# When the gate and up weights of the next feed-forward tiles are asked for

## The chip, the cores and the metric

The kernel runs on one core of a Trainium2 chip. A core has a matmul engine (PE, with its weight loads shown apart as PEld), a vector engine (DVE), a scalar engine (ACT), a general-purpose engine (POOL), and a queue processor (SP) that here only issues DMAs. The metric is device time in microseconds (us), the median of several runs. All arithmetic is on 4-byte floats; large matmuls are done in three parts (high by high, high by low, low by high) of operands that were split into a high and a low part.

## The reference

One transformer block over 2048 rows of 512 features, with modulation vectors made from a condition `c`:

```
mod = silu(c) @ w_mod                      # six vectors of 512: sa, ca, ga, sb, cb, gb
h = layernorm(x) * (1 + ca) + sa
x = x + ga * (softmax(q k^T / 4) v) @ wo   # 32 heads of 16 features, q, k, v = h @ wqkv
h = layernorm(x) * (1 + cb) + sb
x = x + gb * (silu(h @ w_gate) * (h @ w_up)) @ w_down    # 512 -> 1792 -> 512
```

## The kernel before, in words

The 2048 rows are cut into four chunks of 512. First q, k and v are projected. Then attention runs over 32 units: a unit is one chunk of query rows (4) by one group of four heads (8), in 16 steps of 128 keys. For each step PE computes four score blocks (L573), ACT takes their exponentials (L575), and PE multiplies them with v (L588, "pv"). Beside that, 21 steps ahead, PE computes the scores once more in another orientation (L524) and DVE takes their row maxima (L526); one score block and one maximum block form a "pair" in `pair_of`. The finished maxima of a unit go into two rows of its query operand `qop` by eight small DMAs (L563, `qop<-turned`) or two (L542, `qop<-mr`), and the unit's first score needs them.

When a unit ends, `close_unit` sends off its sum row (L599, `dn<-o`), and asks for the keys and queries of the unit three further on (L448, `kop<-kd` and `qop<-qd`, one half from SP's queue and one from POOL's). Some steps later the reciprocal goes out (L604, `d_dr<-dn`), comes back spread over partitions (L609, `rb<-d_dr`), and POOL multiplies it in (L614).

When all eight units of a chunk are done, the chunk's output projection, second layer norm and feed-forward follow, mixed into the attention of the next chunk. For chunks 0 to 2 this is done by `filled_tile` and `filled`: they issue 16 (or 8) pairs and between them, by a table of places, the matmuls of one feed-forward tile; behind the pairs stands a block of pv matmuls. The feed-forward has 14 gate-and-up tiles of 128 features (`gate_up`, 0 to 13) and 7 pairs of down tiles (`down`). The order of the jobs is gate_up 0, 1, 2, two downs, gate_up 3, 4, two downs, 5, 6, and so on to 13. A gate-and-up tile is 48 matmuls in row halves (L790 in `accumulate`). Its weights, high and low parts together, are 1 MB, and were written to DRAM in that form earlier.

The tile `wgu` that holds these weights has two buffers in turn (`tile_gu`, `bufs=2`); the two tiles of output-projection weights (`load_wo`) use the same two. `load_gu(f)` takes the next buffer and issues the DMA `wgu<-gu_dr` from SP's queue (L718); it does nothing where tile f was already asked for:

```
def load_gu(self, f):
    if f < NF and f not in self.loaded:
        self.loaded.add(f)
        self.w[f] = self.places[f % len(self.places)] if self.places else tile_gu()
        nc.sync.dma_start(self.w[f].bitcast(F32), gu_dr[f])
```

The DMA waits, on SP, until the last matmul that read the buffer's earlier contents has ended; whatever SP has behind it in program order waits too. Each engine runs its instructions in the order in which this program writes them. `gate_up(ch, f, ...)` begins with `ch.load_gu(f + ch.ahead)`, and `ahead` is 1 for chunks 0 to 2; `scaled`, which starts the second layer norm, loads tile 0. The last chunk runs alone at the end, with `ahead` 4 and more buffers, and with whole rows instead of halves. The down weights (`load_wd`, L723, 1 MB) have one buffer and are asked for at the end of the second down of the pair before.

Of the kernel before, what the change touches and what calls it, by code (L numbers as in the profile page):

```python
# [104 lines left out]
def block_kernel(ctx, tc, x, wqkv, wo, w_gate, w_up, w_down, c, w_mod, out):  # L105
# [526 lines left out]
    def tile_mid():  # L632
        return pf.tile([P, 2, CW], F32R, name="mid", tag="mid", bufs=3)

    def tmp(name):
        return pf.tile([P, CW], F32, name=name, tag="tmp", bufs=4)
# [142 lines left out]
    def accumulate(outs, lhs, rhs, nk, after, halves, by_k=False, trade=False):  # L779
        ends = []  # L780


        terms = [(k, a, b) for k in range(nk) for a, b in ((0, 0), (0, 1), (1, 0))]
        z = len(terms) - 1
        if halves:
            for ph in range(2):
                for j, (k, a, b) in enumerate(terms):
                    for e in (ph, 1 - ph):
                        rows = slice(64 * (ph ^ e), 64 * (ph ^ e) + 64)
                        mm = nc.tensor.matmul(outs[e], lhs(e, a, k)[rows], rhs(b, k)[rows],  # L790
                                              start=(ph == 0 and j == 0), stop=(j == z and (ph == 1 or trade)),
                                              skip_group_check=(ph == 1 and trade))
                        if trade and j == z * (1 - ph):
                            if ph == 0:
                                ends.append(mm.ins.name)
                            else:
                                tc.add_manual_dep(mm.ins, seen.ins.name, SYNC, reason="row halves trade banks")
                    if trade and j == z and ph == 0:
                        seen = nc.scalar.nop()
                        for name in ends:  # L800
                            tc.add_manual_dep(seen.ins, name, SYNC, reason="row halves trade banks")
                    if j == z and ph:
                        after()
                    yield
        else:
            order = [(e, j) for e in range(2) for j in range(z + 1)]
            for e, j in sorted(order, key=lambda o: o[1] // 3) if by_k else order:
                k, a, b = terms[j]
                nc.tensor.matmul(outs[e], lhs(e, a, k), rhs(b, k), start=(j == 0), stop=(j == z))  # L809
                if e == 1 and j == z:  # L810
                    after()
                yield
# [42 lines left out]
    def gate_up(ch, f, outs, halves, trade=False):  # L855
        ch.load_gu(f + ch.ahead)
        if f == 0:
            ch.load_wd(0)
        ch.mid[f] = mid = tile_mid()

        def after():
            th = tmp("th")
            nc.scalar.activation(th, outs[0], AF.Tanh, scale=0.5)  # L863

            def later():
                q = tmp("q")
                nc.vector.scalar_tensor_tensor(q, th, 1.0, outs[0], op0=ALU.add, op1=ALU.mult)  # L867
                m32 = tmp("m32")
                nc.vector.tensor_mul(m32, outs[1], q)  # L869
                slow = halves or (ch.ci, f) == (last - 1, NF - 2)  # L870
                (nc.gpsimd.tensor_copy if slow else nc.scalar.copy)(mid[:, 0, :], m32)  # L871
                (nc.gpsimd if slow else nc.vector).tensor_sub(mid[:, 1, :], m32, mid[:, 0, :].bitcast(F32))  # L872
            posts.append(later)

        w = ch.w.pop(f)
        return accumulate(outs, lambda e, a, k: w[:, 2 * e + a, k, :], lambda b, k: ch.hT[b][:, k, :], NK, after,
                          halves, trade=trade)
# [29 lines left out]

    def scaled(ch):
        ch.load_gu(0)
        ch.norm_scale(nc.gpsimd)  # L910
        ch.nt = [tile_mid().bitcast(F32) for _ in range(2)]
        for t in range(4):
            ch.normalize(t)
# [65 lines left out]
    halves = [(i, half) for i in range(n) for half in range(2)]  # L979
# [118 lines left out]
    for ci in range(last):  # L1098
        plain(STARTS[ci] - done // 4)
        ch = chunks[ci]  # L1100
        for t0 in (0, 2):
            filled_tile(out_pair, ch, t0)
        behind.append([6, lambda: scaled(ch)])
        tails = [None] * 10
        for k in range(NK):
            tails += [lambda tp, k=k: ch.turned(tp, k), None, None]
        plain(NORM, tails)
        if ci == last - 1:
            plain(REST)
        for _ in range(len(ch.jobs) - (KEEP if ci == last - 1 else 0)):  # L1110
            job, args = ch.jobs.pop(0)
            if ci == last - 1 and args == (7,):
                plain(18 - REST)
            if job is gate_up:
                filled_tile(job, ch, *args)
            else:
                filled(DOWN, job(ch, *args, outs, True))
# [25 lines left out]
    ch, chp = chunks[last], chunks[last - 1]  # L1143
# [54 lines left out]
```

## Time and profile before

| | us |
|---|---|
| median of 3 runs | 1848.37 (1847.08 to 1849.05) |
| the profiled execution, its own time | 1851.1 |
| span of its trace, first to last instruction | 1849.3 |
| PE busy | 1815.8 (98% of the span) |
| DVE busy | 1508.7 (82%) |
| ACT busy | 1234.1 (67%) |
| POOL busy | 459.3 (25%) |
| mean granted clock of PE | 0.991 |

Times in the trace count from the span's start. The chain of waits follows the work that ended last backwards; its shares say which engine or DMA held the end at each moment. In the tables of stretches each row is one stretch of time: its length, the busy time of each engine with the number of its instructions in brackets, the clock granted to PE (1.00 is full), the share of the 16 DMA engines in use, and GB/s. Matmuls on the two row halves run side by side, so PE starts more of them than their single durations would allow. In this profile the landings of DMAs issued by SP are not listed; when a load has landed is seen from the instruction that waited for it, or from the DMA share.

### The profile page before, as it was taken

The page shows a single profiled execution, that of the slowest core. Times are in us where ns is not written, and L with a number is a line of the kernel's source. Part 1 is how long each engine was busy: PE and PEld are TensorE (multiplying, and loading weights), DVE is VectorE, ACT ScalarE, POOL GpSimd, SP SyncE. Part 2 cuts the span into 40 slices and gives each one's busy share as a digit, 9 for nine tenths or more (in the row PEclk, how much of TensorE's full clock was granted, in tenths as well). Part 3 has the DMA queues.
Part 4 walks back from the last instruction along what each step waited for, and adds up shares of the span by engine and source line. Part 5 has one row for each costly group of instructions (what it writes and reads, how often), then busy time and mean ns, then how long its engine had stood idle before and what let it go on. Part 6 is the DMA issues. An engine that isn't in the chain of part 4 may idle for free.

```text
span 1849.3 us, 41033 instructions
## 1 busy us (share of the span) xinstructions
PE 1815.8 (98%) x16892; PEld 1180.7 (64%) x16892; DVE 1508.7 (82%) x2558; ACT 1234.1 (67%) x2356; POOL 459.3 (25%) x538
## 2 busy tenths in 40 slices
PE   9999999999999899989999899989999999999999
PEld 7876444444464677767564677767564577677887
DVE  6478999999999788878999788878999988932543
ACT  4223888888888666656788666656788876774211
POOL 3622544655223111111133111111123111130200
PEclk9999999999999999989999999999999999999999
DMA  9784866677645444445445444445443555233642
GB/s 310 277 236 139 215 182 164 175 183 197 190 77 121 99 122 109 113 111 139 107 121 120 99 107 122 115 110 141 105 121 79 130 118 137 109 121 121 267 171 109
DMA packets 80704, 267.63 MB, mean 145 GB/s; under 512 B 19884, under 2 KB 24428, under 8 KB 59836
## 3 DMA queue, kind: packets, MB, share of 16 engines
q1 hardware_dynamic: 61540, 179.71, 33.4%
q0 software_dynamic: 18288, 84.49, 19.0%
q8 instruction: 133, 2.18, 0.5%
q10 hardware_dynamic: 688, 0.80, 0.1%
q14 instruction: 55, 0.45, 0.1%
HBM read 201.85 MB, written 62.13 MB: 143 GB/s over the span
## 4 chain that ended last, share of the span: by engine, by line
PE 79%; DVE 14%; DMA 5%; ACT 1%; issue 0%; SPq 0%; DVEq 0%; ACTq 0%
PE bank L588 20%; PE bank L790 19%; DVE mx L526 14%; PE bank L573 13%; PE bank L524 11%; PE bank L809 8%; PE bank L214 7%; DMA wgu<-gu_dr 4%; PE bank L852 1%; DMA dn<-o 1%; DMA wm_ab<-in_w_mod 1%; PE bank L773 0%; PE bank L166 0%; DVE v_flat L883 0%; ACT o L592 0%
## 5 line engine op out<-in xcount | busy, mean ns | idle before, releaser
L526 DVE TENSOR_REDUCE mx<-bank 128x1 f32<-128x512 f32 x2048 | 1261.1, 681 | 146.8 <-PE bank L524 81.5
L573 PE MATMUL bank<-qop,kop 50*128 50x512 f32 x2048 | 735.5, 429 | 2.2 <-ACT pu__13024 L575 0.5
L524 PE MATMUL bank<-kop,qop 48*128 48x512 f32 x2048 | 728.5, 427 | 1.0 <-DVE mx L526 0.5
L573 PEld LDWEIGHTS bank<-qop,kop 50*128 50x128 f32 x2048 | 348.3, 185 | 195.8 <-issue 35.3
L524 PEld LDWEIGHTS bank<-kop,qop 48*128 48x128 f32 x2048 | 348.8, 186 | 111.1 <-DVE mx L526 67.6
L790 PE MATMUL bank<-act,wgu 64*128 64x512 f32 x1872 | 314.7, 402 | 21.5 <-DMA wgu<-gu_dr 21.5
L790 PEld LDWEIGHTS bank<-act,wgu 64*128 64x128 f32 x1872 | 195.9, 192 | 42.4 <-issue 23.1
L614 POOL TENSOR_TENSOR rb<-o,rb 128x512 f32<-128x512 f32 x31 | 39.8, 1285 | 430.1 <-DMA rb<-d_dr 378.9
L871 POOL CAST mid<-m 128x512 fp32r<-128x512 f32 x40 | 24.2, 606 | 475.1 <-DVE m L869 475.1
L790 PE MATMUL bank<-wd,mid 64*128 64x512 f32 x912 | 131.1, 391 | 0.0
L790 PEld LDWEIGHTS bank<-wd,mid 64*128 64x128 f32 x912 | 91.0, 186 | 12.1
L214 PE MATMUL bank<-hT,wqs 128*128 128x512 f32 x384 | 94.3, 397 | 0.4 <-DVE wqs L354 0.4
L214 PEld LDWEIGHTS bank<-hT,wqs 128*128 128x128 f32 x384 | 70.6, 188 | 18.9 <-issue 3.0
L867 DVE SCALAR_TENSOR_TENSOR q<-th,bank 128x512 f32<-128x512 f32 x56 | 37.8, 676 | 54.5 <-ACT th L863 54.5
L863 ACT ACTIVATE th<-bank 128x512 f32<-128x512 f32 x56 | 33.5, 598 | 58.7 <-PE bank L809 58.5
L883 DVE TENSOR_TENSOR x<-bank,x 128x512 f32<-128x512 f32 x84 | 53.9, 685 | 16.1 <-PE bank L790 16.1
L869 DVE TENSOR_TENSOR m<-bank,q 128x512 f32<-128x512 f32 x56 | 38.7, 692 | 21.4 <-PE bank L809 19.4
L872 POOL TENSOR_TENSOR mid<-m,mid 128x512 fp32r<-128x512 f32 x40 | 51.3, 1282 | 3.4
L809 PE MATMUL bank<-wd,mid 128*128 128x512 f32 x216 | 51.3, 393 | 0.0
L214 PE MATMUL bank<-wqs,hT 128*128 128x512 f32 x192 | 48.0, 398 | 0.0
L790 PE MATMUL bank<-wgu,act 64*128 64x512 f32 x288 | 47.8, 392 | 0.0
L809 PEld LDWEIGHTS bank<-wd,mid 128*128 128x128 f32 x216 | 40.4, 188 | 8.9
(6300 smaller groups left out, 5140.9 us busy)
## 6 DMA issues: line engine op xcount, KB each, us to landing
wgu<-gu_dr SPq DMA_DIRECT2D x48, 1024.0 KB
wd<-wd_dr SPq DMA_DIRECT2D x28, 1024.0 KB
kop<-kd SPq DMA_DIRECT2D x33, 768.0 KB
kop<-kd POOLq DMA_DIRECT2D x29, 768.0 KB, 8.6
gu_dr<-wgu POOLq DMA_DIRECT2D x14, 1024.0 KB, 13.5
kd<-prt SPq DMA_DIRECT2D x16, 512.0 KB
qd<-prt SPq DMA_DIRECT2D x16, 512.0 KB
kop<-gu_dr SPq DMA_DIRECT2D x8, 1024.0 KB
```

The source lines that it names most:

```text
L214: nc.tensor.matmul(pt, lhs(a, k), rhs(b, k), start=(n == 0), stop=(n == 3 * nk - 1))
L524: nc.tensor.matmul(pm, qop[u][rows, s, qt * P:(qt + 1) * P], kop[u % 3][rows, s, kc * CW:(kc + 1) * CW], start=True, stop=True)
L526: nc.vector.tensor_reduce(mx[u][:, b, s, qt, kc:kc + 1], pm, op=ALU.max, axis=AX.X)
L573: nc.tensor.matmul(sp, kop[u % 3][rows, h // 2, kt * P:(kt + 1) * P], qop[u][rows, h // 2, :], start=True, stop=True)
L588: nc.tensor.matmul(pv[u][32 * h:32 * h + 32, cols], v_flat[:, e0:e0 + 32], p_[h][:, cols], start=(kt == 0 and half == 0), stop=(kt == 15), ...
L614: mul.tensor_mul(rb, o, rb)
L790: mm = nc.tensor.matmul(outs[e], lhs(e, a, k)[rows], rhs(b, k)[rows], start=(ph == 0 and j == 0), stop=(j == z and (ph == 1 or trade)), sk ...
L809: nc.tensor.matmul(outs[e], lhs(e, a, k), rhs(b, k), start=(j == 0), stop=(j == z))
L867: nc.vector.scalar_tensor_tensor(q, th, 1.0, outs[0], op0=ALU.add, op1=ALU.mult)
L869: nc.vector.tensor_mul(m32, outs[1], q)
L872: (nc.gpsimd if slow else nc.vector).tensor_sub(mid[:, 1, :], m32, mid[:, 0, :].bitcast(F32))
L883: nc.vector.tensor_add(ch.x2[:, t, :], outs[e], ch.x2[:, t, :])
```

## The change

In the tiles that are done in row halves (chunks 0 to 2), `after`, which is called when the last matmul of tile f has been issued, first asks for tile f + 2. That load takes the buffer that tile f has just read. `scaled` asks for tile 1 right behind tile 0. The call at the head of `gate_up` stays; in these chunks it finds its tile already asked for. The number of loads and of all other instructions stays the same.

```
--- before
+++ after
@@ gate_up
         ch.mid[f] = mid = tile_mid()
 
         def after():
+            if halves:
+                ch.load_gu(f + 2)
             th = tmp("th")
             nc.scalar.activation(th, outs[0], AF.Tanh, scale=0.5)
...
@@ scaled
     def scaled(ch):
         ch.load_gu(0)
+        ch.load_gu(1)
         ch.norm_scale(nc.gpsimd)
```

The first place that the prediction speaks of is the start of chunk 0's feed-forward in SP's queue. The weight loads are `wgu<-gu_dr`, the down weights `wd<-wd_dr`, and `kop`/`qop` the keys and queries of a later unit. Before (tile 0's load is the row ahead of these):

```order
L599 DMA dn<-o 128x1x16
L448 DMA kop_88<-kd 48x2x2048
L448 DMA qop<-qd 48x2x512
L604 DMA d_dr<-dn 128x16
L609 DMA rb<-d_dr 128x1x512
L718 DMA wgu<-gu_dr 128x2048
L723 DMA wd<-wd_dr 128x2048
L563 DMA qop<-turned 2x8x32 x8
L599 DMA dn<-o 128x1x16
L448 DMA kop_971<-kd 48x2x2048
L448 DMA qop<-qd 48x2x512
L718 DMA wgu<-gu_dr 128x2048 x2
```

And now:

```order
L718 DMA wgu<-gu_dr 128x2048 x2
L599 DMA dn<-o 128x1x16
L448 DMA kop_88<-kd 48x2x2048
L448 DMA qop<-qd 48x2x512
L604 DMA d_dr<-dn 128x16
L609 DMA rb<-d_dr 128x1x512
L723 DMA wd<-wd_dr 128x2048
L563 DMA qop<-turned 2x8x32 x8
L718 DMA wgu<-gu_dr 128x2048
L599 DMA dn<-o 128x1x16
L448 DMA kop_971<-kd 48x2x2048
L448 DMA qop<-qd 48x2x512
```

Tile 1's load has moved up to tile 0's, away from the place ahead of `wd`. Tile 2's load has moved from behind `dn<-o`, `kop_971<-kd` and `qop<-qd` (where it stood with tile 3's) to ahead of them, right behind the eight small writes.

The second place is the middle of chunk 0's feed-forward in the same queue, between the loads of tiles 6 and 10. Before:

```order
L718 DMA wgu<-gu_dr 128x2048 x2
L563 DMA qop<-turned 2x8x32 x8
L599 DMA dn<-o 128x1x16
L448 DMA kop_88<-kd 48x2x2048
L448 DMA qop<-qd 48x2x512
L723 DMA wd<-wd_dr 128x2048
L718 DMA wgu<-gu_dr 128x2048
L604 DMA d_dr<-dn 128x16
L609 DMA rb<-d_dr 128x1x512
L718 DMA wgu<-gu_dr 128x2048
L563 DMA qop<-turned 2x8x32 x8
```

And now:

```order
L718 DMA wgu<-gu_dr 128x2048
L563 DMA qop<-turned 2x8x32 x8
L718 DMA wgu<-gu_dr 128x2048
L599 DMA dn<-o 128x1x16
L448 DMA kop_88<-kd 48x2x2048
L448 DMA qop<-qd 48x2x512
L723 DMA wd<-wd_dr 128x2048
L604 DMA d_dr<-dn 128x16
L718 DMA wgu<-gu_dr 128x2048
L609 DMA rb<-d_dr 128x1x512
L718 DMA wgu<-gu_dr 128x2048
L563 DMA qop<-turned 2x8x32 x8
```

In the first of these two pieces the loads are those of tiles 6 and 7 together, then 8, then 9; in the second they are those of tiles 7, 8, 9 and 10. Tile 10's load, which before came only after the next `kop<-kd`, is now ahead of the second block of eight small writes.

More of the change, by code (lines that the diff above doesn't have):

```diff
@@ L861, in after @@
         def after():
+            if halves:
+                ch.load_gu(f + 2)
             th = tmp("th")
@@ L909, in scaled @@
         ch.load_gu(0)
+        ch.load_gu(1)
         ch.norm_scale(nc.gpsimd)
```

## The prediction

> **What bounds the kernel now.** I read the page first, then the waits, then the chain of waits, then tables of stretches around what they point at.
>
> ```profile
> span 1849.3 us, 41033 instructions
> ...
> PE 1815.8 (98%) x16892; PEld 1180.7 (64%) x16892; DVE 1508.7 (82%) x2558; ACT 1234.1 (67%) x2356; POOL 459.3 (25%) x538
> ...
> PE 79%; DVE 14%; DMA 5%; ACT 1%; issue 0%; SPq 0%; DVEq 0%; ACTq 0%
> PE bank L588 20%; PE bank L790 19%; DVE mx L526 14%; PE bank L573 13%; PE bank L524 11%; PE bank L809 8%; PE bank L214 7%; DMA wgu<-gu_dr 4%; PE bank L852 1%; DMA dn<-o 1%; DMA wm_ab<-in_w_mod 1%; PE bank L773 0%; PE bank L166 0%; DVE v_flat L883 0%; ACT o L592 0%
> ```
>
> PE is busy for all but 33.5 us of the span, and 79% of the chain is PE's own work. The one DMA with a share to speak of is the load of gate and up weights, 4%. The waits say what PE loses to it:
>
> ```profile
> PE bank L790 <- DMA wgu<-gu_dr: 21.5, 4, 5.7
> ```
>
> Four waits, 21.5 us together, the longest 5.7: nearly two thirds of all of PE's idle time. The other loads of this kind cost PE nothing. The first of the four, in SP's timeline and (the last two rows) in the chain:
>
> ```profile
> 615.95 0.60 SPq L599 DMA_DIRECT2D dn<-o  x1
> 616.66 0.42 SPq L448 DMA_DIRECT2D kop<-kd  x1
> 617.16 0.38 SPq L448 DMA_DIRECT2D qop<-qd  x1
> 617.64 7.58 SPq L718 DMA_DIRECT2D wgu<-gu_dr  x2
> ...
> 617.64 16.82 DMA wgu<-gu_dr
> ...
> 634.60 1.65 PE bank L790 x6
> ```
>
> Tile 2's weights are asked for at 617.64, behind a unit's keys and queries, and take 16.82 us to land. PE starts the tile at 634.60. The other three waits are tile 10 of chunk 0 and tiles 2 and 10 of chunk 1, the places where a unit closes just before the load is issued. In chunk 2 the units close at other points.
>
> The wait is not all that is lost. This table of 2 us stretches has PE's granted clock in the third column from the right:
>
> ```profile
> 630.00:632.00 2.00, 0.00 (x0) 0.00 (x0) 0.47 (x1) 0.23 (x1) 0.00 (x0) 1.00 0.96 358
> 632.00:634.00 2.00, 0.00 (x0) 0.00 (x0) 0.00 (x0) 0.00 (x0) 0.00 (x0) 0.67 0.99 414
> 634.00:636.00 2.00, 1.40 (x6) 1.24 (x8) 0.00 (x0) 0.00 (x0) 0.00 (x0) 0.50 0.52 217
> 636.00:638.00 2.00, 2.00 (x12) 1.69 (x10) 0.73 (x2) 0.60 (x2) 0.00 (x0) 0.50 0.01 4
> 638.00:640.00 2.00, 2.00 (x14) 1.64 (x14) 1.41 (x3) 1.28 (x3) 0.00 (x0) 0.62 0.00 0
> 640.00:642.00 2.00, 2.00 (x20) 1.40 (x18) 1.92 (x4) 1.67 (x4) 0.00 (x0) 1.00 0.00 0
> ```
>
> While PE waits, its clock falls to half, and it comes back only some 5 us after PE has resumed: 12 matmuls start in 2 us where 20 do at the full clock.
>
> **The change part by part.** What a stall costs in all is read from equal pieces of work: from the start of the tile ahead of the stall to the start of the first down behind the stalled tile, that is two gate-and-up tiles with their pairs and pv blocks. The four stalled pieces and two clean ones (the second and third row):
>
> ```profile
> 615.78:650.18 34.40, 29.15 (x292) 21.08 (x289) 22.95 (x38) 18.77 (x36) 4.85 (x7) 0.90 0.55 127
> 663.79:690.50 26.71, 26.71 (x291) 19.24 (x288) 22.47 (x37) 18.97 (x36) 4.82 (x6) 1.00 0.62 135
> 744.44:771.06 26.62, 26.62 (x290) 19.46 (x288) 22.97 (x41) 18.53 (x36) 5.02 (x6) 1.00 0.44 143
> 784.67:820.11 35.44, 29.76 (x290) 21.60 (x288) 22.94 (x38) 18.78 (x36) 3.58 (x4) 0.86 0.56 138
> 1031.62:1066.27 34.65, 29.41 (x291) 21.43 (x288) 22.85 (x37) 18.77 (x36) 4.85 (x7) 0.90 0.56 126
> 1201.61:1236.59 34.98, 29.67 (x290) 21.57 (x288) 22.94 (x37) 18.77 (x36) 3.57 (x4) 0.90 0.56 138
> ```
>
> All hold 290 to 292 matmuls. A clean piece takes 26.7 us with PE busy throughout; the stalled ones take 7.7, 8.7, 7.9 and 8.3 us more, **32.6 us** together: 21.5 of waiting and 11.1 of half clock. In a clean piece DVE is busy for 22.9 of 26.7 us and ACT for 19.0, so PE stays the bound when the stall is gone, and DVE has 3.8 us to spare.
>
> The Trainium skill (TensorE: Matmul & The Clock Gate, Part 1) says that after an idle window of about 3.4 us PE runs at half clock, and prices this as the throttled time times one half. The mean clocks 0.90, 0.86, 0.90 and 0.90 above make 30.7 us of throttled time, so by that rule 15.4 us on top of the 21.5, or 36.9, and the median would become 1811.5. The trace agrees on the half clock; it gives 11.1 because part of each slow stretch lies inside the wait, where nothing is slowed.
>
> *Tile 2's load*, now asked for at the end of tile 0. When that is, and when tile 8 of chunk 0 ends, which now releases tile 10's load, is in the rows of L790 for these two tiles (first and last start):
>
> ```profile
> L790 PE MATMUL bank<-act,wgu x48: 384/392/399, 602.3 to 611.1; 64*128 64x512 f32 x48
> ...
> L790 PE MATMUL bank<-act,wgu x48: 385/392/400, 757.7 to 766.4; 64*128 64x512 f32 x48
> ```
>
> Tile 0 has ended by 611.5, so the load is issued then instead of at 617.64, and goes ahead of the keys. It is needed when tile 1 has run its course, half a clean piece after 615.8, at 615.8 + 13.3 = 629.1. Its length has two bounds. Alone, a load moves like tile 0's, issued at 564.51:
>
> ```profile
> 564.00:566.00 2.00, 2.00 (x26) 0.93 (x26) 2.00 (x5) 1.87 (x5) 0.00 (x0) 1.00 0.37 61
> 566.00:568.00 2.00, 2.00 (x31) 0.90 (x22) 1.93 (x6) 1.65 (x5) 0.25 (x2) 1.00 0.88 344
> 568.00:570.00 2.00, 2.00 (x24) 0.90 (x18) 2.00 (x5) 1.71 (x5) 1.41 (x8) 1.00 0.31 131
> ...
> 610.00:612.00 2.00, 2.00 (x24) 1.57 (x24) 2.00 (x5) 1.90 (x4) 0.00 (x0) 1.00 0.00 0
> 614.00:616.00 2.00, 2.00 (x30) 1.20 (x24) 0.23 (x1) 0.66 (x2) 1.91 (x3) 1.00 0.00 0
> ```
>
> 2 us times (61 + 344 + 131) GB/s is the 1 MB: it is over by 570, about 5 us. Behind a unit's keys it took 16.82. So it lands between 616.5 and 628.3; even the late end is 0.8 us ahead of the need. I take 5 to 6 us, since the last two rows show the DMA engines empty where it now goes. *Tile 10's load* is released at 766.4 + 0.4 and needed, one clean tile behind 784.67, at 798: with 16.8 us it would still be 14 us early. Chunk 1 has the same order. So all four waits go, and with them the half clock: -32.6, with an end of -21.5 if the slow clock had another cause.
>
> *Tile 1's load* moves beside tile 0's at a chunk's start. It adds 5 us of DMA ahead of `dn<-o`, `kop` and `qop`, and takes 5 us away ahead of `wd`. Nothing waits on the first three there, and the rows above show the engines drained by 570; cost 0, and at most the same 5 us, three times, if a keys' load were just in time, which no wait on `kop` or `qop` by PE shows.
>
> *The other loads* of tiles 3, 7, 9 and 11 are issued where they were, those of 4, 5, 6, 8, 12 and 13 earlier, ahead of keys, `rb` or `wd`. PE waited for none of them; what they are put ahead of can come at most one load, 5 us, later. Keys have time (no wait of PE on them), `wd` is asked for two gate-and-up tiles, 26.7 us, before its down: 0.
>
> *What SP now holds up.* A load that waits for its tile's last matmul holds whatever is behind it. Behind tile 4's and tile 12's loads stands `rb<-d_dr`, which then lands some 5 us later. POOL waits for it; its next work:
>
> ```profile
> 651.06 1.30 POOL L614 TENSOR_TENSOR rb<-o,rb 128x512 f32<-128x512 f32 x1 [0.75 <-DMA rb<-d_dr]
> ...
> 675.26 0.60 POOL L871 CAST mid<-m 128x512 fp32r<-128x512 f32 x1 [22.01 <-DVE m L869]
> ```
>
> 22 us of idle POOL cover that; 0. Without that cover 5 us would fall on `mid` and the downs. The eight writes L563 are tighter, since a unit's first score needs them:
>
> ```profile
> SPq L563 <- DMA wgu<-gu_dr: 3.7, 6, 1.8
> ...
> 1079.99 6.10 SPq L563 DMA_DIRECT2D qop<-turned  x8
> ...
> 1087.47 0.47 PE L573 MATMUL bank<-qop,kop 50*128 50x512 f32 x1 [0.52 <-ACT pu__13024 L575]
> ```
>
> Here the writes waited 1.8 us for tile 4's load just ahead, ended at 1086.1, and the score behind them came 0.5 us late. In the change that load is asked for a tile earlier and only `wd` stands ahead of the writes: 0.5 won back. Two places a chunk (tiles 7 and 10, in chunk 2 four) keep a load just ahead of the writes, as before the change; with 5 us a load they are where they were, 0.
>
> **Sum**: 32.6 + 0.5 = 33.1. The profiled execution took 1851.1 for a span of 1849.3, so its successor should take 1818.0. The median is 2.7 below that execution: 1848.4 - 33.1 = **1815.3 us**, 1.8% faster.
>
> **The rivals.**
>
> *The slow clock stays (0.04).* Then only the waits go: 1848.4 - 21.5 - 0.5 = 1826.4. For it: no row names the cause of the half clock. Against it is the mean over the whole span:
>
> ```profile
> core 0: 1849.3 us, clock 0.991
> ```
>
> The four pieces lack 0.10 x 34.40 + 0.14 x 35.44 + 0.10 x 34.65 + 0.10 x 34.98 = 15.4 us of clock, 0.008 of the span. That leaves 0.001 for all the rest, so the slow clock comes with the stalls only.
>
> *Only tile 10's waits go (0.04).* Tile 2's load has only tile 1's time to land, and the 0.8 us at the late end is thin. If keys delay it all the same, 7.7 + 7.9 stay: 1815.3 + 15.6 = 1830.9. Against it: it is now ahead of the keys.
>
> *The gain is given back (0.02).* A later stage with DVE as its bound could absorb time: the chain has 14% on L526. Then the time is near 1848. Against: DVE works on what PE has written, so its work moves forward with PE's.
>
> *Slower (0.03).* SP's queue becomes the bound through the eight writes. Eight times in the three chunks they stand right behind a load, and SP already waits in such loads:
>
> ```profile
> SPq L718 <- PE bank L573: 78.2, 10, 11.0
> ```
>
> If those loads took 16.8 instead of 5 us, each unit's first score would come 16.8 - 5 - 1.4 (1086.1 to 1087.47) = 10.4 us late: 83 us in all. It decides from 33.1 / 8 = 4.1 us a place; at half the places the time is 1815.3 + 42 = 1857. Against: at the same places a load stands ahead of the writes already, and the six waits there come to 3.7 us. The Trainium skill (DMA: Bandwidth & Descriptors, Anatomy of one DMA) speaks for this rival: DMA engines do not wait on semaphores, the issuing sequencer does, before dispatch. The 78.2 us agree.
>
> **How the numbers follow.** The forecast holds 0.87. With the rivals, faster by over 0.2% (about what a measurement of this kernel tells from no change) is 0.95, within it 0.02, slower 0.03. The forecast's own range is 1811.5 to 1819, by the half clock's price and the run's spread; the first rival widens it to 1828. The second and the rest, 0.09, stay out.
>
> **What would show it.** Right: no wait of L790 on `wgu<-gu_dr`, a mean clock of 0.99 to 1.00 with no stretch at half inside the feed-forwards, the tile pairs at 26.7 us, tile 2's load issued within 1 us of tile 0's end. Wrong: waits of L573 behind L563, L871 late behind L614, or a clock that still falls to half.

## The result, and the profile after

| | median, us | from to, runs |
|---|---|---|
| before | 1848.26 | 1847.08 to 1849.05, 6 |
| after | 1818.11 | 1816.22 to 1820.13, 6 |

The ratio is 0.9838, with a 95% interval of 0.9825 to 0.9851: 30.2 us less. The forecast was 1815.3, with a range of 1811.5 to 1828. The profiled execution of the changed kernel took 1817.3, where the forecast for it was 1818.0.

The page of the changed kernel, the lines that answer to those of before:

```profile
span 1815.5 us, 41028 instructions
...
PE 1804.4 (99%) x16892; PEld 1171.6 (65%) x16892; DVE 1508.9 (83%) x2558; ACT 1233.2 (68%) x2356; POOL 458.9 (25%) x538
...
PE 86%; DVE 12%; DMA 1%; ACT 1%; issue 0%; SPq 0%; DVEq 0%
...
L790 PE MATMUL bank<-act,wgu 64*128 64x512 f32 x1872 | 305.7, 392 | 0.0
```

PE's idle time fell from 33.5 to 11.1 us, and DMA from 5% of the chain to 1%. The last line, of the costliest groups, is the one to look at (busy time, mean duration in ns, idle time of PE ahead of it). The same line of the page of before:

```profile
L790 PE MATMUL bank<-act,wgu 64*128 64x512 f32 x1872 | 314.7, 402 | 21.5 <-DMA wgu<-gu_dr 21.5
```

The idle time of PE ahead of gate-and-up matmuls, 21.5 us before, is 0.0. The same 1872 matmuls also take 392 ns in the mean instead of 402: that is the half clock that is gone. Over all its work PE is busy for 11.4 us less (1815.8 to 1804.4), close to the 11.1 us of half clock in the prediction's sum.

SP's timeline of the changed kernel at the first of the four places, and (last row) the mean granted clock of the whole span:

```profile
610.70 0.33 SPq L718 DMA_DIRECT2D wgu<-gu_dr  x1
615.18 0.61 SPq L599 DMA_DIRECT2D dn<-o  x1
615.84 0.46 SPq L448 DMA_DIRECT2D kop<-kd  x1
616.35 0.42 SPq L448 DMA_DIRECT2D qop<-qd  x1
624.08 0.34 SPq L718 DMA_DIRECT2D wgu<-gu_dr  x1
...
core 0: 1815.5 us, clock 1.000
```

Tile 2's load now leaves at 610.70, as tile 0's last matmul ends, 4.5 us ahead of SP's next DMA. How long it takes is seen from the DMA engines (the last two columns, share in use and GB/s), which were empty until then:

```profile
608.00:610.00 2.00, 2.00 (x20) 1.56 (x18) 2.00 (x5) 1.80 (x4) 0.00 (x0) 1.00 0.00 0
610.00:612.00 2.00, 2.00 (x32) 1.28 (x32) 2.00 (x4) 1.85 (x4) 0.00 (x0) 1.00 0.36 61
612.00:614.00 2.00, 2.00 (x44) 1.23 (x40) 0.96 (x2) 0.00 (x0) 0.78 (x2) 1.00 0.77 295
614.00:616.00 2.00, 2.00 (x25) 1.36 (x17) 1.01 (x2) 1.44 (x3) 2.00 (x3) 1.00 0.42 176
```

2 us times (61 + 295 + 176) GB/s is about its 1 MB, so it is over by about 616. The four pieces of work that were stalled before, each again from the start of the tile ahead to the start of the down behind:

```profile
615.00:641.68 26.68, 26.68 (x292) 19.31 (x288) 22.68 (x38) 18.63 (x36) 4.82 (x7) 1.00 0.71 156
776.18:802.86 26.68, 26.68 (x290) 19.34 (x288) 22.57 (x37) 18.56 (x36) 3.55 (x4) 1.00 0.73 173
1014.32:1041.01 26.69, 26.69 (x290) 19.24 (x288) 22.55 (x38) 18.56 (x36) 4.81 (x7) 1.00 0.72 155
1175.62:1202.34 26.72, 26.72 (x291) 19.27 (x289) 22.57 (x38) 18.62 (x36) 3.57 (x4) 1.00 0.74 173
```

All four take the 26.7 us of a clean piece, at full clock.

### The profile page after: what moved, and what is told of

Read it like the earlier page. It is cut to its first block, busy times and chain, and to the rows that moved or that the text cites. A ratio compares the mean times of both kernels' runs of the same rounds, so it can differ in the third digit from the quotient of the medians.

```text
span 1815.5 us, 41028 instructions
## 1 busy us (share of the span) xinstructions
PE 1804.4 (99%) x16892; PEld 1171.6 (65%) x16892; DVE 1508.9 (83%) x2558; ACT 1233.2 (68%) x2356; POOL 458.9 (25%) x538
## 4 chain that ended last, share of the span: by engine, by line
PE 86%; DVE 12%; DMA 1%; ACT 1%; issue 0%; SPq 0%; DVEq 0%
PE bank L588 22%; PE bank L790 20%; PE bank L573 15%; PE bank L524 12%; DVE mx L526 12%; PE bank L809 8%; PE bank L214 7%; PE bank L852 1%; DMA wm_ab<-in_w_mod 1%; PE bank L773 1%; PE bank L166 0%; DMA qop<-mr 0%; DVE v_flat L885 0%; PE bank L538 0%; SPq L255 0%
## 5 line engine op out<-in xcount | busy, mean ns | idle before, releaser
L524 PEld LDWEIGHTS bank<-kop,qop 48*128 48x128 f32 x2048 | 346.1, 184 | 109.0 <-DVE mx L526 66.4
L790 PE MATMUL bank<-act,wgu 64*128 64x512 f32 x1872 | 305.7, 392 | 0.0
L790 PEld LDWEIGHTS bank<-act,wgu 64*128 64x128 f32 x1872 | 190.3, 186 | 17.9
L790 PE MATMUL bank<-wd,mid 64*128 64x512 f32 x912 | 131.3, 391 | 0.0
L790 PEld LDWEIGHTS bank<-wd,mid 64*128 64x128 f32 x912 | 91.3, 186 | 11.8
L865 ACT ACTIVATE th<-bank 128x512 f32<-128x512 f32 x56 | 33.5, 598 | 58.4 <-PE bank L809 58.2
L885 DVE TENSOR_TENSOR x<-bank,x 128x512 f32<-128x512 f32 x84 | 53.9, 685 | 16.1 <-PE bank L790 16.1
L790 PE MATMUL bank<-wgu,act 64*128 64x512 f32 x288 | 47.7, 392 | 0.0
```

What stands on the lines that cost most here:

```text
L524: nc.tensor.matmul(pm, qop[u][rows, s, qt * P:(qt + 1) * P], kop[u % 3][rows, s, kc * CW:(kc + 1) * CW], start=True, stop=True)
L885: nc.vector.tensor_add(ch.x2[:, t, :], outs[e], ch.x2[:, t, :])
```

## The experiments

Times are compared with the kernel before on the same chip: 1848.9 for the first four, 1847.3 for the next four, 1848.1 for the last three.

**The parts of the change.** Each one alone:

```
last_slot_only:  the change without    +  ch.load_gu(1)   in scaled
tile1_only:      of the change only    +  ch.load_gu(1)   in scaled
tile2_only:      of the change only    +  if halves and f == 0:  ch.load_gu(f + 2)
tile10_only:     of the change only    +  if halves and f == 8:  ch.load_gu(f + 2)
```

> Only the load at the last slot of each tile, without asking for tile 1 beside tile 0. My theory (the gain is the four waits for tiles 2 and 10 and the half clock behind them): all of the gain, 32 to 33 us, some 1816 to 1818, no wait of L790 on wgu. The rival that asking for tile 1 early matters: less gain by 5 us or more, with a wait left at tile 1 or 2.

> Only tile 1 beside tile 0 at a chunk's start, the rest as before. My theory: no gain, 1848 within 1 us, the four waits stay as they are (5.2 to 5.7 us each). Rival: tile 2's waits get shorter because tile 1's load is out of the way, 1848 less up to 15 us.

> The load at the last slot for tile 0 alone, so only tile 2 is asked for early. My theory: the two waits of tile 2 go with their half clock, 7.7 + 7.9 = 15.6 us, some 1832.7; tile 10's two waits stay. If stalls only moved on to the next place: 1848.

> The load at the last slot for tile 8 alone, so only tile 10 is asked for early. My theory: the two waits of tile 10 go, 8.7 + 8.3 = 17.0 us, some 1831.3, and this gain and that of tile 2 alone add up to that of the whole change within 1.5 us. If they hide each other: a sum well off 32.6.

| | median, us | ratio to before, 95% interval |
|---|---|---|
| last slot only | 1817.8 | 0.983 (0.9816 to 0.9845) |
| tile 1 only | 1849.4 | 1.000 (0.999 to 1.001) |
| tile 2 only | 1832.8 | 0.9913 (0.9898 to 0.9927) |
| tile 10 only | 1831.7 | 0.9908 (0.9893 to 0.9923) |

The load at the last slot is the whole gain; asking for tile 1 beside tile 0 is worth nothing, as expected. The early loads of tile 2 and of tile 10 bring 16.1 and 17.2 us, 33.3 together against 31.1 for all tiles on the same chip. The sum is 2.2 us off, more than the 1.5 that I had allowed, but the 95% interval of each of these gains reaches some 2.7 us either way. Within that the gains add, and no other load is seen to matter. The stalls that were left in the two partial kernels (two pieces of tile 2 only, then two of tile 10 only) show something else:

```profile
776.10:808.86 32.76, 28.35 (x291) 20.46 (x289) 22.70 (x37) 18.57 (x36) 3.58 (x4) 0.95 0.59 148
1182.35:1217.06 34.71, 29.37 (x291) 21.38 (x288) 22.82 (x38) 18.75 (x36) 3.56 (x4) 0.90 0.58 141
```
```profile
614.14:648.25 34.11, 28.96 (x292) 21.03 (x289) 22.92 (x38) 18.77 (x36) 4.82 (x7) 0.90 0.56 128
1020.95:1054.77 33.82, 28.67 (x291) 20.83 (x288) 22.82 (x38) 18.67 (x36) 4.83 (x7) 0.90 0.57 130
```

They cost 6.1, 8.0, 7.4 and 7.1 us over a clean piece: 28.6 together, where the same four cost 32.6 in the trace of before. The waits differ little (PE waited 9.7 and 10.3 us in these two traces, 20.0 together, against 21.5); the stretch of half clock varies more. At the first of them the mean clock was 0.95, at the same place before 0.86.

**Was the load asked for too late, or only behind the wrong thing?** In this kernel the weights are asked for as before, but the keys go behind them at the four unit ends.

```
 in close_unit, for u in (10, 13, 18, 21):
-    load_k(u + 3); load_q(u + 3)
+    at(i + 3, lambda: (load_k(u + 3), load_q(u + 3)))
```

> The kernel before, with weights asked for when they were, but at the four unit ends ahead of the stalls the next keys and queries (L448) are asked for three steps later, behind the weight load. If the load was late because the keys stood ahead of it: the load lands about 5 us after its issue at 616 to 617, the four waits go, 1815 to 1818. If one tile of lead is too short by itself: the waits stay, 1848.

Measured: 1820.4, ratio 0.9856 (0.9842 to 0.9871). In SP's timeline of this kernel, and its waits (last row):

```profile
615.34 0.42 SPq L718 DMA_DIRECT2D wgu<-gu_dr  x1
615.81 0.42 SPq L448 DMA_DIRECT2D kop<-kd  x1
616.28 0.58 SPq L448 DMA_DIRECT2D qop<-qd  x1
...
PE bank L790 <- DMA wgu<-gu_dr: 1.3, 3, 0.8
```

One exchange of rows in a queue takes 27 us off, although the load leaves hardly earlier than before (0.7 us behind `dn<-o`, where it was 1.7). But my reason was only half right. I expected it to land in 5 us; PE still waited for such loads three times, 1.3 us in all, and at the first of them the tile began at 628.21, 12.9 us after the issue, where it took 16.8 before. The keys' other half goes through POOL's queue at the same moment (it left at 614.51), and SP ran on and issued its own half at once, since nothing made it wait three steps. So the load shared the DMA engines from its first moment, where the change has them to itself for over 4 us (POOL's half leaves there at 615.05).

**Is the half clock a price of PE standing idle?** Here the kernel before gets extra matmuls ahead of the four stalled tiles, whose results the tile overwrites.

```
 in gate_up:
+    if halves and ch.ci < 2 and f in (2, 10):
+        for _ in range(24):        # 12 in the second kernel
+            nc.tensor.matmul(outs[0], ch.hT[0][:, 0, 0:P], ch.hT[0][:, 0, :], start=True, stop=True)
```

> The kernel before, with 24 extra matmuls of 128x512 (about 5.2 us at full clock) ahead of tiles 2 and 10 of chunks 0 and 1, into a bank that the tile then starts anew. They fill PE's wait for the weights. If the half clock comes from PE standing idle: clock 1.00 throughout, each stalled piece 5.3 to 6 us longer than a clean one instead of 7.7 to 8.7, some 1837 to 1839. If it comes from something else (the DMA load, say): the half clock stays and the time is 1848 or above.

> As with 24, but 12 extra matmuls (2.6 us), so that PE still waits about 2.8 us at each of the four places. If only a wait longer than about 3 us costs the clock: as with 24, 1837 to 1839. If any wait of some us does: the half clock stays, some 1847 to 1849.

| | median, us | ratio to before, 95% interval |
|---|---|---|
| 24 extra matmuls | 1841.8 | 0.9967 (0.9955 to 0.9979) |
| 12 extra matmuls | 1841.4 | 0.9971 (0.9958 to 0.9983) |

Work that nobody needs made the kernel faster. The first stalled piece with 24 of them:

```profile
615.67:648.24 32.57, 32.57 (x314) 23.46 (x312) 22.80 (x38) 18.64 (x36) 4.80 (x7) 1.00 0.60 135
```

PE is busy throughout, the clock stays at 1.00, and the piece is 5.9 us over a clean one instead of 7.7. So at these places it is PE's idleness that costs the clock, and not the DMA load. The time is 3 to 4 us above the 1837 to 1839 that I had expected. I had counted from a time without stalls of 1848.4 - 32.6 = 1815.8, and the changed kernel measures 1817.5 to 1818.1; four times 5.9 on top of 1817.5 makes 1841.1. So the 32.6 us were too much for a usual execution, and the half clock, at these places and elsewhere, is what varies: of the ten runs of tile 1 only, which keeps all four stalls, two with a mean clock of 0.990 took 1851.7 and 1852.4 us, two with 0.994 1846.1 and 1846.9. The trace of before had 0.991, most other runs of that kernel 0.992 to 0.994. With 12, where about 2 us of waiting are left, stretches around the wait read:

```profile
630.00:632.00 2.00, 1.81 (x9) 0.89 (x8) 0.36 (x1) 0.39 (x1) 0.00 (x0) 1.00 0.94 385
632.00:634.00 2.00, 0.21 (x2) 0.22 (x4) 0.93 (x2) 0.69 (x2) 0.00 (x0) 1.00 1.02 430
634.00:636.00 2.00, 2.00 (x16) 1.59 (x16) 0.80 (x2) 0.67 (x2) 0.00 (x0) 0.84 0.12 49
636.00:638.00 2.00, 2.00 (x12) 1.58 (x10) 1.27 (x2) 1.12 (x2) 0.00 (x0) 0.50 0.00 0
```

Here PE was idle for some 2 us, and the clock fell only after PE had resumed. It did so at one of the four places; at the three others PE stood idle 1.1 to 1.7 us and the clock stayed. The time is that of 24, as expected if only longer waits cost the clock, but my line of about 3 us was too high. Other executions of this kernel took up to 1846.4 us, with a mean clock down to 0.996, so there more was lost.

**Does SP's waiting cost anything?** In the changed kernel the last-slot loads are issued by POOL.

```
-    ch.load_gu(f + 2)
+    ch.load_gu(f + 2, nc.gpsimd)      # load_gu takes the issuing engine
```

> The changed kernel, with the loads at the last slot issued by POOL instead of SP, so that nothing of SP's queue stands behind their wait. If SP's waiting cost something in the change: faster than it by what it cost, 1 us or more. My theory is that it costs nothing: 1818 within 1.5 us, or some us slower where POOL's own work (the casts of mid) comes late behind the 0.6 us of each issue.

Measured: 1817.0, ratio 0.984 (0.9826 to 0.9855), the changed kernel's time. POOL now waits 290 us in these loads and it does not matter either; the holding of a queue is free in these two kernels, as costed.

**How far is the slower rival?** At the eight places where a weight load stands just ahead of the eight small writes, the same load is issued once or twice more. SP is held until each has landed before it issues the next.

```
 in after, behind the new call:
+    if f + 2 in ((7, 10), (7, 10), (2, 5, 8, 9))[ch.ci]:
+        for _ in range(1):         # 2 in the second kernel
+            nc.sync.dma_start(ch.w[f + 2].bitcast(F32), gu_dr[f + 2])
```

> The changed kernel once more, beside the two below on one chip. 1816 to 1820. If the half clock still falls somewhere in single runs (PE idle for a moment outside the feed-forwards), runs with a mean clock of 0.998 are 2 to 3 us longer than runs with 1.000.

> The changed kernel; at the eight places where a weight load stands just ahead of the eight small writes of qop's maxima (tiles 7 and 10 of chunks 0 and 1; 2, 5, 8, 9 of chunk 2) the same load is issued a second time behind the first, so SP is held about 5 us longer and the last write goes some 5 us later. The margin between the last write's landing and the unit's first score is 4 to 6 us in the changed kernel's trace. If this margin is what keeps the change from the slower rival: 0 to 1 us lost at a place, some 4 us in all, 1822. If the writes have far more room: no loss. If SP's queue is already the bound: 5 us at each place, 40 us.

> As twice, with the load issued three times at the eight places: the last write some 10 us later. By the margin of 4 to 6 us: 4 to 6 us of PE waiting at each place, some 41 us in all, 1859, and up to 1880 with the half clock behind the longer waits; that is slower than the kernel before. If the writes have far more room: 1818.

| | median, us | ratio to before, 95% interval |
|---|---|---|
| the changed kernel once more | 1817.5 | 0.9835 (0.9817 to 0.9852) |
| each load twice | 1820.4 | 0.9851 (0.9835 to 0.9866) |
| each load three times | 1883.8 | 1.0192 (1.0174 to 1.021) |

The first repeats the result; its runs all had a mean clock of 1.000. Other runs tell what 0.998 costs: the one of the changed kernel took 1820.1 us, where its two with 1.000 took 1817.3 and 1818.4, and with POOL as the issuer one took 1819.9 against 1816.6 and 1816.7. That is 2 to 3 us, as expected, though it rests on two runs. A second load loses 2.9 us, a third 66.4, twice the gain of the change. The writes of the changed kernel beside tile 7's load, then the same place with three loads (in SP's timeline, then the unit's first score in PE's and the wait in total, and at the end what happened at tile 10, in POOL's timeline and in the chain):

```profile
704.68 0.31 SPq L718 DMA_DIRECT2D wgu<-gu_dr  x1
706.21 4.39 SPq L563 DMA_DIRECT2D qop<-turned  x8
```
```profile
706.85 0.32 SPq L718 DMA_DIRECT2D wgu<-gu_dr  x1
712.23 5.40 SPq L866 DMA_DIRECT2D wgu<-gu_dr  x2
717.72 4.95 SPq L563 DMA_DIRECT2D qop<-turned  x8
...
723.92 0.76 PE L573 MATMUL bank<-qop,kop 50*128 50x512 f32 x1 [5.74 <-DMA qop<-turned]
...
PE bank L573 <- DMA qop<-turned: 50.6, 7, 10.1
...
781.76 0.57 POOL L448 DMA_DIRECT2D kop<-kd  x1 [8.52 <-PE bank L524]
...
782.74 8.33 DMA qop<-turned
```

The second trace is 2.2 us behind the first already at the load. Counted from the load, the writes begin 10.9 us behind it instead of 1.5, that is 9.3 us later, and end 9.9 us later; the first score waits for them. Of the 66.4 us, 50.6 are such waits, at seven places. The rest is that PE is busy 16.1 us longer (1820.7 against 1804.6), mostly by the half clock behind the waits (mean clock 0.984). So the margin is real and narrow: some 5 us more ahead of the writes is nearly hidden, 10 us more turns the change into the slower rival. My 41 us were too low, though the last write went 10 us later as expected. At tile 7 the wait is 5.74 us, as the margin has it. At tile 10 it is 10.1: there the last write left 1 us behind POOL's half of the next keys and took 8.33 us to land, where at tile 7 the score follows 1.25 us behind the end of the writes. That the keys made it slow is argued from these two rows, not tested. With the half clock I had said up to 1880.

## Why the prediction was right, point by point

**What bounds the kernel.** Right. PE waits for four loads, and nothing took their place: the four pieces are clean, and the change's chain has 1% of DMA.

**The loads of tiles 2 and 10.** Right, and the partial kernels show that these two are the whole gain. Of my bounds for the landing, 5 to 16.8 us, the early one held, by the DMA rows from 610 to 616. So the second rival, in which tile 2's waits stay, is out. That the keys ahead of the load cost most of the 30 us is shown by the kernel in which only they changed places. Why they cost it, by sharing the DMA engines, is read from the times, and the half in POOL's queue counts too.

**Tile 1's load.** Costed at nothing; alone it measured 1.000 (0.999 to 1.001).

**The half clock.** Its mechanism was right: matmuls put into the waits keep the clock at 1.00. So the first rival, that it would stay, is out. Its size is where the sum went wrong. The step was "32.6 us together: 21.5 of waiting and 11.1 of half clock", which the sum takes off the median, though "the median is 2.7 below that execution" in which they were read. That execution, slower than the three runs beside it, was slow in part because its stalls were dear. Taken off the same execution the sum came out well: 1818.0 against 1817.3. The four stalls together cost 28.6 us in the traces of the two partial kernels. By 28.6 + 0.5 the forecast would have been 1819.3; the measured 1818.1 lies between the two. That the median came out within 3 us is also luck in part, since one execution cannot tell a usual price. "So the slow clock comes with the stalls only" held for that trace, but not for every one, as the last section shows. The rule of the Trainium skill that I weighed (TensorE: Matmul & The Clock Gate, Part 1), half of the throttled time on top of the waits, would have given 1811.5 and was further off, for the reason given: part of each slow stretch lies in the wait.

**The small gain of 0.5 us.** At that place the changed kernel's writes are no longer held (its SP timeline):

```profile
1051.83 0.32 SPq L723 DMA_DIRECT2D wd<-wd_dr  x1
1054.73 4.36 SPq L563 DMA_DIRECT2D qop<-turned  x8
...
1061.50 0.60 ACT L575 ACTIVATE pu__13024<-bank 128x512 f32<-128x512 f32 x1
...
1061.51 0.44 PE L573 MATMUL bank<-qop,kop 50*128 50x512 f32 x1
```

4.36 us for the eight instead of 6.10, and the score (the last row) starts without the 0.52 us of idle time. The row of before names the exponential `pu__13024` as what ended that wait; here the same score starts as this exponential starts, so it does not need it, and the reading that it had waited for the writes holds. A median cannot show 0.5 us, so its effect on the time is not measured.

**What SP holds up.** Costed at nothing, and right: `rb` came while POOL had time, and with POOL as the issuer the time was the same. The list of tiles had one slip: tile 9's load, said to be issued where it was, now also stands ahead of an `rb` (744.98 and 745.47 in SP's timeline of the changed kernel). POOL waited 3.70 us for it and was idle for another 5.90 us behind it, so this cost nothing either. The slower rival is a true mechanism; it was kept off by the 5 us that a load takes where the DMA engines are free, as the kernel with three loads shows. The gain was not given back in a later stage: all four pieces gained, and the time of the whole fell by as much.

## What to carry to other kernels

A load that is late need not have been asked for too late: look first at what stands ahead of it in its queue, since here moving the load ahead of two rows brought 27 of the 30 us. Cost a wait of PE by equal pieces of work, from before the wait to well behind it, and from several executions, because the half clock behind the wait is part of the price and varies from run to run. Before a load is moved up, find the small urgent DMA that will stand behind it and measure its margin by issuing the load twice and three times.

## What the runs showed of the hardware

The half clock does not follow from the length of a wait alone. Waits of 5 to 6 us were followed by mean clocks of 0.95 to 0.86 over the same piece of work. With 12 extra matmuls a wait of some 2 us cost the clock at one of four places, while three of 1.1 to 1.7 us did not. At that one place the clock fell when PE was already at work again.

It can also come without such a wait. The trace of last slot only has no wait of L790 on `wgu<-gu_dr`, and yet a mean clock of 0.999. The place is behind chunk 2's output projection:

```profile
1398.00:1400.00 2.00, 1.71 (x22) 0.69 (x22) 1.94 (x5) 1.67 (x4) 0.61 (x1) 1.00 0.00 0
1400.00:1402.00 2.00, 2.00 (x12) 0.89 (x10) 1.66 (x5) 1.73 (x4) 0.00 (x0) 1.00 0.34 131
1402.00:1404.00 2.00, 2.00 (x18) 0.72 (x18) 2.00 (x4) 1.32 (x3) 0.00 (x0) 0.64 0.02 3
1404.00:1406.00 2.00, 2.00 (x14) 1.03 (x14) 1.34 (x3) 1.02 (x3) 0.00 (x0) 0.50 0.03 4
```

PE is idle for 0.3 us and then starts only 12 matmuls in 2 us, after 22. The changed kernel's trace has the same idle time there and 11 matmuls, and keeps the full clock. So a stretch of thin work can bring the half clock in one execution and not in the next; what decides it is not shown.
